# Reciprocal decays from one reciprocal and a backward scan, in a linear-attention, MLP and expert kernel

## The chip, the cores and the metric

One core of a Trainium2 chip runs the whole program. The metric is the device time of one execution in microseconds (us); lower is better. PE is TensorE (matmul), PEld its weight loads, DVE is VectorE, ACT is ScalarE, POOL is GpSimd, SP is the engine that issues most of the DMA transfers.

## The reference

The attention part keeps a state per head and decays it by `w` at every position; two feed-forward parts follow. Only the first part is touched by the change.

```
for t in range(S):                       # S = 768, batch 4, 8 heads, 48 wide
    kt, vt, rt, wt = (k[:, :, t], v[:, :, t], r[:, :, t], w[:, :, t])
    cur = np.einsum('bhd,bhe->bhde', u[None] * kt, vt)
    y[:, :, t] = np.einsum('bhd,bhde->bhe', rt, state + cur)
    state = wt[:, :, :, None] * state + np.einsum('bhd,bhe->bhde', kt, vt)
...
h = x @ w_in                             # 3072 x 384 times 384 x 2048
x = (np.maximum(h, 0.0) + alpha * np.minimum(h, 0.0)) @ w_out
...                                      # then the best of 8 experts per token: relu(x @ w1) @ w2, times its gate weight
```

## The kernel before, in words

**Attention by tiles.** The 3072 tokens are 24 tiles of 128 positions, six to a batch element. Inside a tile the recurrence is turned into matmuls: with the running product of decays `ex` (one per position, head and channel), `r` is multiplied by `ex`, `k` is divided by the `ex` of the position behind it, and the masked product of the two gives the scores. The 112 partitions of `dm` are two heads of 48 channels with a gap of 16, and along each partition lie four head pairs: 512 values of `r`, 512 of `k` and then `w` as four runs of 129, the first of each run being 0, so that one scan over 516 values starts anew in every run.

For a tile DVE does `scan` (L277, writes `ex`), `rec0` (L301, the reciprocal of every fourth `ex`), `rec1` (L305, three multiplications that get the other three of four, each from the one behind it times `w`), and `k` (L307, `k` times `rec`). POOL does `r` (L292, `r` times `ex`), the product `rk` (L312 and then L313), the masks of the scores (L360), and further on `cv` (L328) and the state's decay (L395). DVE sums `rk` to `c` (L318), adds `y` and `cv` to `x` (L424), and splits `x` into a high and a low part (L446 writes the low one, `xtl`).

**Blocks.** Three tiles make a block of 384 tokens for the first MLP: 16 steps, each nine matmuls into `ph` (L584, of which two buffers exist), ACT's `gn` (L587), DVE's `gt` (L589), ACT's `gh` (L595), DVE's `gl` (L597) and nine matmuls into `py` (L610). While a block goes through its 16 steps, the tiles of the next block are done between them.

**Weights.** `w_in` and `w_out` arrive as 64-bit words in 16 pieces. Each piece takes three DVE instructions of 768 columns (L207, L208, L211), two of ACT (L203, L224), and a subtraction for the low part (L229, on DVE for even pieces, which writes `wil`, on POOL for odd ones, `wol`). This work runs in the prologue and in the first MLP block alone.

**What sets the order.** The prologue (tiles 0 to 2 and the first pieces of weights) is written out by hand for all engines, by a table of times (`PRO_OPS`, `PRO_MOVED`) that gives nothing but an order. From the first MLP step on only PE's order is written by hand; a scheduler that estimates durations orders DVE, ACT, POOL and SP. From six steps before the last MLP step on, DVE's order is by hand as well.

Of the kernel before, what the change touches and what calls it, by code (L numbers as in the profile page):

```python
# [9 lines left out]
F32 = mybir.dt.float32  # L10
# [16 lines left out]
NP = H // 2  # L27
PR = 112
KC = DM // 128
NF1 = DFF // 128  # L30
# [32 lines left out]
OPS = {  # L63
# [6 lines left out]
PRO_OPS = {  # L70
# [3 lines left out]
}  # L74
PRO_NEXT = ("scan", "rec0", "rec1", "k", "r", "rk")
PRO_MOVED = {
# [6 lines left out]
}  # L83
# [13 lines left out]
def attention_mlp_moe(ctx, tc, dmaj, tmaj, ub, alpha, w_in, w_out, w_gate, w_gate_b, wexp, out):  # L97
# [23 lines left out]
    def load_tile(i):  # L121
        if i < NB:
            both = wp.tile([128, 1540 + 3 * DM], F32, tag="W", name="both")
            dm, tm = both[:PR, :1540], both[:, 1540:].rearrange("p (c d) -> p c d", c=3)
            if i == 0:
                sp.dma_start(out=dm[:, 1024:], in_=dmaj[i, :, 1024:])
                sp.dma_start(out=dm[:, :1024], in_=dmaj[i, :, :1024])
            else:
                sp.dma_start(out=dm, in_=dmaj[i])
        else:  # L130
            dm = ap.tile([PR, 1540], F32, tag="dm", name="dm")
            tm = ap.tile([128, 3, DM], F32, tag="tm", name="tm")
            sp.dma_start(out=dm, in_=dmaj[i])
# [19 lines left out]
    pool.memset(apat, 0.0)  # L153
    pool.memset(apat[:, :, 0:1], 1.0)
    ident = cst.tile([128, 128], F32, name="ident")
    make_identity(nc, ident)
# [108 lines left out]
    def att_tile(i, s0):  # L265
# [8 lines left out]
        def scan():  # L274
# [3 lines left out]
                out=ex.rearrange("p a t -> p (a t)"),  # L278
                data0=dm[:, 1024:1540],
                data1=apat.rearrange("p a t -> p (a t)"),  # L280
# [7 lines left out]
            cx["v"] = tm_t[i][:, 2, :]  # L288
            cx["rec"] = ap.tile([PR, NP, 128], F32, tag="rec", name="rec", bufs=1)

# [3 lines left out]
        def rec(n):  # L294

            def at4(t, m):
                return t.rearrange("p a (g m) -> p a g m", m=4)[:, :, :, m]

            rc, ex = cx["rec"], cx["ex"][:, :, 1:129]
            if n == 0:  # L300
                vec.reciprocal(out=at4(rc, 3), in_=at4(ex, 3))  # L301
            elif n == 1:
                w = dm_t[i][:, 1024:1540].rearrange("p (a t) -> p a t", a=NP)[:, :, 1:129]
                for m in (2, 1, 0):
                    vec.tensor_tensor(out=at4(rc, m), in0=at4(rc, m + 1), in1=at4(w, m + 1), op=ALU.mult)  # L305
            else:
                vec.tensor_tensor(out=cx["k"], in0=cx["k"], in1=rc, op=ALU.mult)  # L307

# [134 lines left out]
        def x_low():  # L443
# [4 lines left out]
        ops = {  # L448
            "scan": scan, "r": decay_r, "rec0": lambda: rec(0), "rec1": lambda: rec(1), "k": lambda: rec(2),
            "rk": diag, "c": diag_sum, "cv": diag_v, "sc": scores,  # L450
# [642 lines left out]
```

## Time and profile before

| | us |
|---|---|
| three timed runs, median (lowest to highest) | 880.32 (878.28 to 882.1) |
| the profiled execution, its own time | 875.71 |
| its span, first to last instruction | 874.0 |
| PE busy, share of the span | 820.5 (94%) |
| DVE busy | 645.4 (74%) |
| ACT busy | 384.3 (44%) |
| POOL busy | 293.4 (34%) |

The shares are means over stages with different limits: a prologue up to about 43 us, the first MLP block with the weights' work up to about 147 us, the other MLP blocks up to about 550 us, and the experts after that. Where an instruction waits inside its engine for something that is not a semaphore, the profile shows it as a longer duration, not as idle time.

### The profile page before, as it was taken

What the parts mean: (1) busy time and instruction counts of PE and PEld (TensorE: products, weight loads), DVE (VectorE), ACT (ScalarE), POOL (GpSimd) and SP (SyncE); (2) the same over time, 40 slices, a digit from 0 to 9 for tenths busy, and PEclk for the clock granted to TensorE, in tenths of its full rate; (3) what the DMA queues carried; (4) which work ended last, traced back from release to release, by engine and by line L of the source; (5) the groups of instructions that cost most, each with busy time, mean ns of one, the idle gap of its engine ahead of it and who ended that gap; (6) DMA issues with size and microseconds to landing.
All of it is one profiled execution on the core that took longest, in us unless ns stands there. A gap on an engine that the chain in (4) does not pass through costs nothing. (4 is left out here: it accounts for less than half of the span.)

```text
span 874.0 us, 14602 instructions
## 1 busy us (share of the span) xinstructions
PE 820.5 (94%) x5453; PEld 796.1 (91%) x5453; DVE 645.4 (74%) x1219; ACT 384.3 (44%) x751; POOL 293.4 (34%) x309
## 2 busy tenths in 40 slices
PE   6878789999799999999999999999999999999994
PEld 4768779999799999999999999999899999999993
DVE  6999898977686996896996983446767576776761
ACT  3545343344133433333333432337355556565641
POOL 5474444233332433343423330122224122232301
PEclk8779888999899999999999999999999999999997
DMA  9625534022212321311312300036456668585830
GB/s 281 203 83 171 193 120 148 29 60 86 59 59 60 87 60 60 86 60 60 86 60 59 87 1 1 28 137 242 147 202 240 224 216 293 204 294 204 275 119 21
DMA packets 30513, 111.59 MB, mean 128 GB/s; under 512 B 8229, under 2 KB 11592, under 8 KB 30440
## 3 DMA queue, kind: packets, MB, share of 16 engines
q1 hardware_dynamic: 26088, 100.38, 35.8%
q0 software_dynamic: 4352, 10.26, 3.2%
q8 instruction: 44, 0.72, 0.3%
q14 instruction: 29, 0.24, 0.1%
HBM read 100.95 MB, written 10.45 MB: 127 GB/s over the span
## 5 line engine op out<-in xcount | busy, mean ns | idle before, releaser
L584 PE MATMUL ph<-xth,wih 128*128 128x384 f32 x384 | 138.1, 360 | 8.4 <-DVE gt L589 5.2
L610 PE MATMUL py<-woh,gh 128*128 128x384 f32 x384 | 138.1, 360 | 1.0 <-ACT gh L595 1.0
L584 PE MATMUL ph<-xth,wil 128*128 128x384 f32 x384 | 132.9, 346 | 6.2 <-DVE wil L229 6.2
L595 ACT CAST gh<-gt 128x384 fp32r<-128x384 f32 x128 | 65.6, 513 | 158.5 <-DVE gt L589 158.5
L610 PE MATMUL py<-woh,gl 128*128 128x384 f32 x384 | 131.4, 342 | 1.4 <-DVE gl L597 1.4
L584 PE MATMUL ph<-xtl,wih 128*128 128x384 f32 x384 | 132.3, 345 | 0.0
L610 PE MATMUL py<-wol,gh 128*128 128x384 f32 x384 | 131.2, 342 | 0.0
L597 DVE TENSOR_TENSOR gl<-gt,gh 128x384 fp32r<-128x384 f32 x128 | 91.9, 718 | 33.3 <-ACT gh L595 31.8
L589 DVE SCALAR_TENSOR_TENSOR gt<-gn,oma_s,ph 128x384 f32<-128x384 f32 x128 | 76.4, 597 | 50.3 <-ACT gn L587 50.1
L587 ACT ACTIVATE gn<-ph 128x384 f32<-128x384 f32 x128 | 62.7, 490 | 113.2 <-PE ph L584 110.1
L815 DVE SCALAR_TENSOR_TENSOR gl<-ph,gh 128x256 fp32r<-128x256 f32 x96 | 40.4, 422 | 73.9 <-ACT gh L813 67.2
L489 DVE SCALAR_TENSOR_TENSOR sink<-x,wgb 128x384 f32<-128x384 f32 x144 | 88.1, 634 | 2.1 <-ACT x L621 1.4
L584 PEld LDWEIGHTS ph<-xth,wih 128*128 128x128 f32 x384 | 74.6, 194 | 10.3 <-DVE gt L589 5.8
L810 PE MATMUL ph<-xh,w1h 128*128 128x256 f32 x288 | 81.5, 283 | 1.2 <-DVE gl L815 1.1
L584 PEld LDWEIGHTS ph<-xth,wil 128*128 128x128 f32 x384 | 74.7, 194 | 7.4 <-DVE wil L229 7.4
L884 POOL DMA_INDIRECT out<-ys,meta x28 | 28.5, 1018 | 156.3 <-ACT ys L881 97.5
L810 PE MATMUL ph<-xl,w1h 128*128 128x256 f32 x288 | 80.8, 281 | 0.0
L810 PE MATMUL ph<-xh,w1l 128*128 128x256 f32 x288 | 80.4, 279 | 0.0
L610 PEld LDWEIGHTS py<-woh,gh 128*128 128x128 f32 x384 | 74.7, 195 | 3.0 <-ACT gh L595 1.3
L610 PEld LDWEIGHTS py<-woh,gl 128*128 128x128 f32 x384 | 74.1, 193 | 2.5 <-DVE gl L597 2.5
L584 PEld LDWEIGHTS ph<-xtl,wih 128*128 128x128 f32 x384 | 74.9, 195 | 0.8 <-DVE xtl L446 0.3
L610 PEld LDWEIGHTS py<-wol,gh 128*128 128x128 f32 x384 | 74.6, 194 | 0.0
(211 smaller groups left out, 1906.4 us busy)
## 6 DMA issues: line engine op xcount, KB each, us to landing
raw<-w SPq DMA_DIRECT2D x64, 768.0 KB
dm<-dmaj SPq DMA_DIRECT2D x21, 673.8 KB
tm<-tmaj SPq DMA_DIRECT2D x21, 576.0 KB
raw<-w_out SPq DMA_DIRECT2D x8, 768.0 KB
raw<-w_in SPq DMA_DIRECT2D x7, 768.0 KB
x2d<-x SPq DMA_DIRECT2D x8, 576.0 KB
both<-tmaj SPq DMA_DIRECT2D x3, 576.0 KB
wgb<-w_gate_b SPq DMA_DIRECT2D x2, 768.0 KB
```

The lines of the kernel that those rows point to most:

```text
L489: vec.scalar_tensor_tensor(out=sink, in0=x2[:, j, :], scalar=1.0, in1=wgb_t[h][:, e, :], op0=ALU.mult, op1=ALU.mult, accum_out=cx["l"][:, ...
L584: pe.matmul(ph, lhsT=w, rhs=x[:, c, :], start=k == 0, stop=k == 3 * KC - 1)
L587: act.activation(gn, ph, AF.Relu, scale=-1.0)
L589: vec.scalar_tensor_tensor(out=gt, in0=gn, scalar=oma_s[:, f : f + 1], in1=ph, op0=ALU.mult, op1=ALU.add)
L595: act.copy(gh, gt)
L597: vec.tensor_tensor(out=gl, in0=gt, in1=gh.bitcast(F32), op=ALU.subtract)
L610: pe.matmul(y_t[blk][j], lhsT=g[:, sl], rhs=w, start=f == 0 and m == 0, stop=f == NF1 - 1 and m == 2,)
L810: pe.matmul(ph, lhsT=w, rhs=x, start=k == 0, stop=k == 3 * KC - 1)
L815: vec.scalar_tensor_tensor(out=gl, in0=ph, scalar=0.0, in1=gh.bitcast(F32), op0=ALU.max, op1=ALU.subtract)
L884: pool.indirect_dma_start(out=out, out_offset=bass.IndirectOffsetOnAxis(ap=d["meta"][:, j, 0:1], axis=0), in_=ys, in_offset=None, bounds_c ...
```

## The change

The other reciprocals of a tile no longer come from every fourth position. One reciprocal of four values (the last `ex` of each of the four runs) goes into a tile `inj` that is zero elsewhere, and a second scan runs from the end to the front: `rec[t] = w[t+1] * rec[t+1] + inj[t]`. It needs `w` one position further, so `dm` grows by one column (1541 instead of 1540). `inj` is filled with zeros once, by POOL, at the start. Where `rec0` and `rec1` stood at two places of the hand-written order, everything is now at that of `rec0`.

```diff
-    "scan": -9, "r": -9, "rec0": -7, "rec1": -5, "k": -3, "rk": -6, "c": 0, "cv": 0, "sc": 0,
+    "scan": -9, "r": -9, "rec0": -7, "k": -3, "rk": -6, "c": 0, "cv": 0, "sc": 0,
...
-    (3, "scan"): 19.55, (3, "rec0"): 19.58, (3, "rec1"): 21.52, (3, "k"): 21.54,
+    (3, "scan"): 19.55, (3, "rec0"): 19.58, (3, "k"): 21.54,
...
+    inj = ap.tile([PR, NP, 129], F32, tag="inj", name="inj", bufs=1)
+    pool.memset(inj, 0.0)
...
             if n == 0:
-                vec.reciprocal(out=at4(rc, 3), in_=at4(ex, 3))
-            elif n == 1:
-                w = dm_t[i][:, 1024:1540].rearrange("p (a t) -> p a t", a=NP)[:, :, 1:129]
-                for m in (2, 1, 0):
-                    vec.tensor_tensor(out=at4(rc, m), in0=at4(rc, m + 1), in1=at4(w, m + 1), op=ALU.mult)
+                vec.reciprocal(out=inj[:, :, 128], in_=ex[:, :, 128])
+                vec.tensor_tensor_scan(
+                    out=rc.rearrange("p a t -> p (a t)")[:, ::-1],
+                    data0=dm_t[i][:, 1025 : 1025 + NP * 129][:, ::-1],
+                    data1=inj.rearrange("p a t -> p (a t)")[:, ::-1],
+                    initial=0.0,
+                    op0=ALU.mult,
+                    op1=ALU.add,
+                )
             else:
-                vec.tensor_tensor(out=cx["k"], in0=cx["k"], in1=rc, op=ALU.mult)
+                vec.tensor_tensor(out=cx["k"], in0=cx["k"], in1=rc[:, :, 1:129], op=ALU.mult)
```

PE's order is the same instruction for instruction. The orders of DVE and POOL move from the first MLP block on, where the scheduler sets them. In the lists below a scan appears as SCALAR_TENSOR_TENSOR, and the lines of the changed kernel are four or five higher (L281 is the forward scan, L302 the reciprocal, L303 the backward scan, L312 `k`, L323 `c`, L429 `x`).

The first place is DVE in the prologue, at tile 3; `x` here is that of tile 1, and `v` is a piece of weights. Before:

```order
L277 SCALAR_TENSOR_TENSOR ex<-dm,apat 112x516
L301 RECIPROCAL rec<-ex 112x128
L424 TENSOR_TENSOR x<-py,cv 128x384
L207 TENSOR_SCALAR v_380<-v_380 128x768
L208 SCALAR_TENSOR_TENSOR v_380<-raw,v_380 128x768
```

In the changed kernel, at the same place:

```order
L281 SCALAR_TENSOR_TENSOR ex<-dm,apat 112x516
L302 RECIPROCAL inj<-ex 112x4
L303 SCALAR_TENSOR_TENSOR rec<-dm,inj 112x516
L429 TENSOR_TENSOR x<-py,cv 128x384
L211 TENSOR_SCALAR v_377<-v_377 128x768
```

The backward scan stands ahead of `x` of tile 1; the three L305 of this tile stood further down, behind `x` of tile 2, and are gone there.

The second place is DVE at the start of the first MLP block, at tile 4; `gt` and `gl` are those of the first MLP step. Before:

```order
L318 TENSOR_REDUCE c<-rk 128x8
L277 SCALAR_TENSOR_TENSOR ex<-dm,apat 112x516
L229 TENSOR_TENSOR wil_119<-v_454,wih_118 128x3x256
L207 TENSOR_SCALAR v_496<-v_496 128x768
L301 RECIPROCAL rec<-ex 112x128
L208 SCALAR_TENSOR_TENSOR v_496<-raw,v_496 128x768
L589 SCALAR_TENSOR_TENSOR gt<-gn,oma_s,ph 128x384
L211 SCALAR_TENSOR_TENSOR v_496<-raw,v_496 128x768
L597 TENSOR_TENSOR gl<-gt,gh 128x384
L207 TENSOR_SCALAR v_537<-v_537 128x768
L305 TENSOR_TENSOR rec<-rec,dm 112x128
```

In the changed kernel, from the same `c` (that of tile 3) on:

```order
L323 TENSOR_REDUCE c<-rk 128x8
L281 SCALAR_TENSOR_TENSOR ex<-dm,apat 112x516
L233 TENSOR_TENSOR wil_121<-v_448,wih_120 128x3x256
L211 TENSOR_SCALAR v_490<-v_490 128x768
L302 RECIPROCAL inj<-ex 112x4
L323 TENSOR_REDUCE c<-rk 128x8
L212 SCALAR_TENSOR_TENSOR v_490<-raw,v_490 128x768
L211 TENSOR_SCALAR v_531<-v_531 128x768
L594 SCALAR_TENSOR_TENSOR gt<-gn,oma_s,ph 128x384
L215 SCALAR_TENSOR_TENSOR v_490<-raw,v_490 128x768
L602 TENSOR_TENSOR gl<-gt,gh 128x384
L212 SCALAR_TENSOR_TENSOR v_531<-raw,v_531 128x768
```

The `c` of tile 4 has come forward, from right behind the MLP's seventh `gt` to right behind the reciprocal: it and the next piece's L211 now stand ahead of the first `gt`. POOL's order is the same up to that point; behind the backward scan, which is the next row, `gt` of the second step follows.

The third place is DVE further on in the first MLP block, ahead of `wil` of the piece that the ninth MLP step needs (the first `c` is that of tile 4, the second that of tile 5). Before:

```order
L589 SCALAR_TENSOR_TENSOR gt<-gn,oma_s,ph 128x384
L208 SCALAR_TENSOR_TENSOR v_742<-raw,v_742 128x768
L318 TENSOR_REDUCE c<-rk 128x8
L211 SCALAR_TENSOR_TENSOR v_742<-raw,v_742 128x768
L597 TENSOR_TENSOR gl<-gt,gh 128x384
L277 SCALAR_TENSOR_TENSOR ex<-dm,apat 112x516
L318 TENSOR_REDUCE c<-rk 128x8
L229 TENSOR_TENSOR wil_739<-v_742,wih_738 128x3x256
```

In the changed kernel, up to the same `wil` (the `c` is that of tile 5):

```order
L323 TENSOR_REDUCE c<-rk 128x8
L212 SCALAR_TENSOR_TENSOR v_734<-raw,v_734 128x768
L602 TENSOR_TENSOR gl<-gt,gh 128x384
L215 SCALAR_TENSOR_TENSOR v_734<-raw,v_734 128x768
L303 SCALAR_TENSOR_TENSOR rec<-dm,inj 112x516
L312 TENSOR_TENSOR dm<-dm,rec 112x512
L211 TENSOR_SCALAR v_772<-v_772 128x768
L233 TENSOR_TENSOR wil_731<-v_734,wih_730 128x3x256
```

The forward scan of tile 5 has left this place for an earlier one, its `c` stands seven rows ahead of `wil` instead of right before it, and the backward scan and `k` of tile 5 stand here instead.

## Rows read from the trace of the kernel before

**Rows 1.** Busy us (x instructions) of PE, PEld, DVE, ACT, POOL; clock; DMA share; GB/s

```profile
12.00:43.00 31.00, 23.73 (x154) 20.48 (x153) 29.38 (x36) 15.25 (x47) 15.47 (x15) 0.75 0.81 245
43.00:147.00 104.00, 84.82 (x470) 80.22 (x469) 97.17 (x120) 48.20 (x89) 54.69 (x50) 0.83 0.41 138
147.00:550.00 403.00, 396.94 (x2656) 387.49 (x2655) 313.20 (x729) 144.64 (x335) 137.51 (x158) 0.99 0.21 61
```

**Rows 2.** PE's waits from 43 to 147 us: total us, times, longest us

```profile
PE ph L584 <- DVE wil L229: 6.2, 3, 5.0
PE ph L584 <- DVE gt L589: 4.5, 1, 4.5
PE px L435 <- DVE x L424: 3.9, 2, 3.4
```

**Rows 3.** Instructions around tile rec, whole span: ns min/median/max, first and last start

```profile
L305 DVE TENSOR_TENSOR rec<-rec,dm x63: 373/391/1402, 39.3 to 507.4; 112x128 f32<-112x128 f32 x63
L301 DVE RECIPROCAL rec<-ex x24: 937/955/957, 5.0 to 503.9; 112x128 f32<-112x128 f32 x24
```

**Rows 4.** Instructions of line 277, the forward scan, in the same columns

```profile
L277 DVE TENSOR_TENSOR_SCAN ex<-dm,apat x21: 1210/1223/1855, 30.7 to 500.4; 112x516 f32<-112x516 f32 x21
```

**Rows 5.** Instructions of line 549, a small reciprocal of the gate

```profile
L549 DVE RECIPROCAL g_meta<-g_se x8: 177/178/179, 177.0 to 622.7; 128x3 f32<-128x3 f32 x8
```

**Rows 6.** Timeline at tile 1: start, us, engine, line [idle before <-releaser]

```profile
13.21 0.96 DVE L301 RECIPROCAL rec<-ex 112x128 f32<-112x128 f32 x1
13.26 1.18 POOL L292 TENSOR_TENSOR both<-both,ex 112x512 f32<-112x512 f32 x1 [1.80 <-DVE ex L277]
...
14.20 2.70 DVE L305 TENSOR_TENSOR rec<-rec,both 112x128 f32<-112x128 f32 x3
...
14.39 1.15 POOL L312 TENSOR_TENSOR rk<-both 128x384 f32<-128x384 f32 x1
15.62 1.03 POOL L313 TENSOR_TENSOR rk<-rk,ub_s 128x384 f32<-128x384 f32 x1
...
17.28 0.68 DVE L307 TENSOR_TENSOR both<-both,rec 112x512 f32<-112x512 f32 x1
...
18.35 0.54 DVE L318 TENSOR_REDUCE c<-rk 128x8 f32<-128x384 f32 x1
```

**Rows 7.** Timeline at tile 3, the last of the prologue's scans

```profile
31.98 0.96 DVE L301 RECIPROCAL rec<-ex 112x128 f32<-112x128 f32 x1
32.03 1.18 POOL L292 TENSOR_TENSOR dm<-dm,ex 112x512 f32<-112x512 f32 x1 [1.19 <-DVE ex L277]
32.85 0.49 DVE L424 TENSOR_TENSOR x<-py,cv 128x384 f32<-128x384 f32 x1
33.16 1.00 POOL L312 TENSOR_TENSOR rk<-tm 128x384 f32<-128x384 f32 x1
...
33.40 0.55 PE L435 MATMUL px<-ident,x 128*128 128x128 f32 x3 [2.02 <-DVE x L424]
```

**Rows 8.** Timeline at tile 4, the start of the first MLP block

```profile
50.27 0.94 DVE L301 RECIPROCAL rec<-ex 112x128 f32<-112x128 f32 x1
...
51.93 0.60 DVE L589 SCALAR_TENSOR_TENSOR gt<-gn,oma_s,ph 128x384 f32<-128x384 f32 x1
...
52.45 4.88 DVE L211 SCALAR_TENSOR_TENSOR v<-raw,v 128x768 uint32<-128x768 uint32 x1
...
54.93 0.99 POOL L313 TENSOR_TENSOR rk<-rk,ub_s 128x384 f32<-128x384 f32 x1
```

**Rows 9.** DVE's groups, 43 to 147 us: busy us, mean ns | idle before <-releaser

```profile
L211 DVE SCALAR_TENSOR_TENSOR v<-raw,v 128x768 uint32<-128x768 uint32 x13 | 19.6, 1511 | 0.0
...
L207 DVE TENSOR_SCALAR v<-v 128x768 uint32<-128x768 uint32 x14 | 9.6, 688 | 0.9 <-ACT v L203 0.8
L305 DVE TENSOR_TENSOR rec<-rec,dm 112x128 f32<-112x128 f32 x12 | 7.2, 597 | 0.1
...
L318 DVE TENSOR_REDUCE c<-rk 128x8 f32<-128x384 f32 x5 | 2.7, 544 | 2.5 <-POOL rk L313 2.5
...
L211 DVE SCALAR_TENSOR_TENSOR v<-spare,v 128x768 uint32<-128x768 uint32 x1 | 1.0, 959 | 0.0
```

More of the change, by code (lines that the diff above doesn't have):

```diff
@@ L28 @@
 PR = 112
+DMW = 2 * 512 + NP * 129 + 1
 KC = DM // 128
@@ L74 @@
 }
-PRO_NEXT = ("scan", "rec0", "rec1", "k", "r", "rk")
+PRO_NEXT = ("scan", "rec0", "k", "r", "rk")
 PRO_MOVED = {
[1 row of a table removed]
[1 row of a table added]
     (2, "sc"): 15.7, (2, "ktr"): 15.82, (2, "a0"): 15.84, (2, "a1"): 15.9, (2, "ko"): 16.0, (1, "cv"): 16.1,
@@ L122, in load_tile @@
         if i < NB:
-            both = wp.tile([128, 1540 + 3 * DM], F32, tag="W", name="both")
-            dm, tm = both[:PR, :1540], both[:, 1540:].rearrange("p (c d) -> p c d", c=3)
+            both = wp.tile([128, DMW + 3 * DM], F32, tag="W", name="both")
+            dm, tm = both[:PR, :DMW], both[:, DMW:].rearrange("p (c d) -> p c d", c=3)
             if i == 0:
@@ L130, in load_tile @@
         else:
-            dm = ap.tile([PR, 1540], F32, tag="dm", name="dm")
+            dm = ap.tile([PR, DMW], F32, tag="dm", name="dm")
             tm = ap.tile([128, 3, DM], F32, tag="tm", name="tm")
@@ L278, in scan @@
                 out=ex.rearrange("p a t -> p (a t)"),
-                data0=dm[:, 1024:1540],
+                data0=dm[:, 1024 : 1024 + NP * 129],
                 data1=apat.rearrange("p a t -> p (a t)"),
@@ L288, in scan @@
             cx["v"] = tm_t[i][:, 2, :]
-            cx["rec"] = ap.tile([PR, NP, 128], F32, tag="rec", name="rec", bufs=1)
+            cx["rec"] = ap.tile([PR, NP, 129], F32, tag="rec", name="rec", bufs=1)
         def decay_r():
@@ L294, in rec @@
         def rec(n):
-            def at4(t, m):
-                return t.rearrange("p a (g m) -> p a g m", m=4)[:, :, :, m]
-            rc, ex = cx["rec"], cx["ex"][:, :, 1:129]
+            rc, ex = cx["rec"], cx["ex"]
             if n == 0:
-                vec.reciprocal(out=at4(rc, 3), in_=at4(ex, 3))
-            elif n == 1:
-                w = dm_t[i][:, 1024:1540].rearrange("p (a t) -> p a t", a=NP)[:, :, 1:129]
-                for m in (2, 1, 0):
-                    vec.tensor_tensor(out=at4(rc, m), in0=at4(rc, m + 1), in1=at4(w, m + 1), op=ALU.mult)
+                vec.reciprocal(out=inj[:, :, 128], in_=ex[:, :, 128])
[7 more added lines that the diff above has]
+                )
             else:
-                vec.tensor_tensor(out=cx["k"], in0=cx["k"], in1=rc, op=ALU.mult)
+                vec.tensor_tensor(out=cx["k"], in0=cx["k"], in1=rc[:, :, 1:129], op=ALU.mult)
         def diag():
@@ L448, in att_tile @@
         ops = {
-            "scan": scan, "r": decay_r, "rec0": lambda: rec(0), "rec1": lambda: rec(1), "k": lambda: rec(2),
+            "scan": scan, "r": decay_r, "rec0": lambda: rec(0), "k": lambda: rec(1),
             "rk": diag, "c": diag_sum, "cv": diag_v, "sc": scores,
@@ L1049, in pairs @@
         return t.reshape(NTILE, 2, D, NP, 128)
-    dmaj = np.zeros((NTILE, PR, 2 * 512 + 516), np.float32)
-    dw = dmaj[:, :, 1024:].reshape(NTILE, PR, NP, 129)
+    dmaj = np.zeros((NTILE, PR, DMW), np.float32)
     dw = np.zeros((NTILE, PR, NP, 129), np.float32)
@@ L1060 @@
         dw[:, sl, :, 1:] = ww[:, j]
-    dmaj[:, :, 1024:] = dw.reshape(NTILE, PR, 516)
+    dmaj[:, :, 1024 : 1024 + NP * 129] = dw.reshape(NTILE, PR, NP * 129)
     def tmj(x):
```

4 rows, old and new, of tables (PRO_MOVED, PRO_OPS) are left out of this document.

## The prediction

> **What bounds the kernel now.** I read the busy times by stage first. From 147 to 550 us PE is busy for 396.94 of 403 us at a granted clock of 0.99; DVE has 90 us to spare there [rows 1]. So whatever the change saves on DVE after about 147 us, 16 of the 24 tiles, is hidden under the matmuls, and no attention is left in the stage of the experts. What can move is the prologue (12 to 43 us, DVE busy 29.38 of 31) and the first MLP block (43 to 147 us, DVE busy 97.17 of 104, PE only 84.82 at a clock of 0.83) [rows 1]. PE's waits in that block name DVE: 6.2 us for `wil`, 4.5 for `gt`, 3.9 for `x` [rows 2].
>
> Then I asked what DVE's 97 us are made of, because the same instruction has very different lengths. L211 takes 0.959 us on one piece and 1.511 on the mean of 13 others; L305 has a median of 391 ns, but a mean of 597 in this block [rows 3, 9]. The timelines show why. L211 at 52.45 us lasted 4.88 us, until just after POOL's chain of `cv`, `rk`, `r` and `rk` was over; its last `rk` ended at 55.92 [rows 8]. At tile 1 the three L305 took 2.70 us, as long as POOL's three instructions beside them, while the reciprocal at 13.21, beside POOL's L292, took its usual 0.96 [rows 6]. So a DVE instruction that reads two tensors from SBUF does not run while POOL works on SBUF, and a reciprocal does. The Trainium skill has this rule (SBUF — State Buffer, section SBUF: two separate sides): DVE and GpSimd share a pair of ports, and whichever starts first holds it for its whole instruction. The trace agrees, with 4.88 us against 0.96.
>
> **What the change removes and adds.** Per tile it removes a reciprocal of 0.955 us (L301) and three L305 of 0.391, 2.13 us together [rows 3]. It adds a reciprocal of four values and a scan over 516. For the first the nearest row is the gate's reciprocal of three values, 0.178 us [rows 5]. For the second it is the forward scan over as many values, 1.223 us [rows 4]. No row shows an instruction that reads backwards. It could cost the same (nothing but the sign of the step differs) or, as an upper bound, twice as much, 2.4 us. I take 1.223, since L305 reads every fourth value and its median of 391 ns shows no such price. Added are then 1.40 us, and 0.73 are saved by durations. Neighbours overlap by about 0.09 us in the timeline (the reciprocal at 50.27 plus 0.94 ends after its follower would have begun, [rows 8]), so two instructions fewer save 0.18 less: **0.55 us per tile**. The memset of `inj`, the column that `dm` gains (4 bytes in 6160) and the longer `rec` are priced at nothing: POOL waits 1.80 us before its first work on tile 1 alone [rows 6], and if that cover were gone they cost some tenths of a us once.
>
> What matters more: the new scan reads two tensors from SBUF, the long reciprocal one. POOL could work under the reciprocal; it can't under the scan.
>
> **Prologue.** At tile 1 L292 starts at 13.26, 0.05 us after the old reciprocal [rows 6]. The new one ends at about 13.21 + 0.18 = 13.39, too late to be first, so the scan waits until L292 ends at 14.44 and runs to about 15.7. L312 follows (1.0, to 16.7), then `k` or L313. `k` can end at 17.3 instead of 17.96, but `c` of tile 1 needs L313, which moves from 16.65 to about 18.3: `c` stays at 18.35 [rows 6], and so does all that DVE does behind it. Taken: 0; bounds -1.7 (the two parts of `rec` shrink from 3.66 to 1.4 plus a wait of at least 0.5) and +0.3. Tile 2 has the same pattern; I take -0.7 for `k`, on which PE waits, bounds -2 and +0.3.
>
> At tile 3 L292 starts at 32.03, again 0.05 after the reciprocal [rows 7]. The scan then waits until 33.21 and ends at about 34.4, and `x` of tile 1, which PE already waits for (2.02 us, [rows 7]), is behind it: 34.3 for 32.85, **+1.4**. If the scan comes first, +0.45. The three L305 that go behind `x` of tile 2 (1.2 us) are worth 0, because the `xtl` behind them waits for the transposes of that very `x` anyhow. Prologue: -0.7 + 1.4 = **+0.7 us**, between -3 and +2.
>
> **First MLP block**, tiles 4 to 7.
> - DVE's own time: 4 x 0.55 = -2.2.
> - Waits of L305 for POOL: 7.2 - 12 x 0.391 = 2.5 us [rows 3, 9], which go. The four new scans wait in their place; POOL is busy 54.69 of 104 us [rows 1], and one of its instructions takes about 1.1 [rows 6, 7]: from 0 to 4 x 1.1 = 4.4, taken 4 x 0.4 = 1.6. Together -0.9.
> - The `c` of tile 4 now stands ahead of the first `gt`, and needs the `rk` that ended at 55.92 [rows 8]. The scheduler believed it ready; the trace says it isn't. DVE gets to it at about 50.27 + 0.18 = 50.5. POOL, undisturbed meanwhile, may be done a us earlier, at 54.9. So DVE idles 4.4 us (3.5 to 5.4) where it lost 4.88 - 0.96 = 3.9 inside L211 before: +0.5. What queues behind it: `gt` of the first step moves from 51.93 to about 54.9 + 0.54 + 0.96 + 0.69 = 57.1 (`c`, a piece's L208 priced as L211, and L207, [rows 9]), and PE, which waited 4.5 us for it, waits about 9.7. PE's 5.2 us are given back if DVE is not behind by then, for PE was to stop 3.4 us for `x` and 5.0 for `wil` further on [rows 2], and both come earlier in DVE's list now: ahead of `x` two L305 and a `gt` less, ahead of `wil` no `c` that has just to wait.
> - That wait for `rk` was 2.5 us [rows 9]; its `c` now has more work ahead of it: -1, between -2.5 and 0.
> - What POOL did under four reciprocals, 4 x 0.955 x 54.69/104 = 2.0 us, it now does at the cost of some other two-tensor instruction: +2.0, between 0 and 3.8.
>
> Block: -2.2 - 0.9 + 0.5 - 1 + 2.0 = **-1.6 us**. With the prologue -0.9 of the profiled 875.71. The timed median is 880.32, 4.6 above the profiled run, so on its scale 879.4; I say **879 us**. A measurement of this kernel can tell about 0.5%, 4.4 us, from no change.
>
> **Rivals.**
> 1. *DVE's list sets the block, and POOL finds other holes* (faster). For it: DVE is in line without a gap for nearly all of 12 to 147 us. Against it: the share of its time that is waiting for POOL. Then the +2.0 falls away, the wait for `rk` goes entirely (-1.5 more), and at tile 3 the scan starts before POOL (+0.45 for +1.4, about -1 more): -0.9 - 2.0 - 1.5 - 1 = -5.4, **875 us**.
> 2. *The wait at `c` of tile 4 stays* (slower). PE's extra 5.2 us are not given back, because `x` and `wil` are late by as much as PE is. It decides from the point where PE reaches the transposes of that `x` later than before: -0.9 + 5.2 = +4.3, **884.6 us**, and more if the `rk` of later tiles repeats it. For it: nothing shortens POOL's chain. Against it: by the bullet above DVE itself is only 0.5 us behind at that place.
> 3. *The backward scan takes twice as long* (slower): 1.2 us more for each of eight tiles, +9.8 on the forecast, **889 us**. Against it: L305's steps. The skill leaves it open (Vector Engine (DVE) Microarchitecture Reference, section 5.1, lists how an operand with a negative step streams as not measured); no run here shows it yet.
>
> **How the numbers follow.** Forecast 0.45, rival 1 0.34, rival 2 0.16, rival 3 0.05. The scheduler's new order from 43 us on makes each of these wide, some 4 us either way. Below the forecast the range takes in rival 1 with that width, to 871. Above it reaches past rival 2, to 886, and leaves out most of rival 3. Faster by over 0.5% is rival 1, 0.34; slower is rivals 2 and 3, 0.21; the rest 0.45.
>
> **What would show it.** Right: the new reciprocal at about 0.18 us; the backward scan at 1.2 where POOL is silent and 2 or more behind L292 at tiles 1 to 3; DVE idle 4 us for POOL's `rk` at about 50 us and PE waiting 9 us for `gt`; the waits for `x` and `wil` shorter; from about 150 us on the same PE time, with DVE some 9 us less busy (16 x 0.55). Wrong: a backward scan of 2.4 us everywhere; scans that start ahead of L292; a first MLP block that is over 4 us shorter or longer; a new wait of PE after 150 us, where the order moved too and I count on none.

## The result, and the profile after

The changed kernel takes **890.55 us** (median of four runs, 889.81 to 891.26) against 879.77 for the kernel before on the same chip: a ratio of **1.0125**, 95% interval 1.0106 to 1.0145, 10.8 us slower. The prediction was 879 us, between 871 and 886, with "no change" as the likeliest. A few executions in a slower state are left out of all medians and ratios.

The profiled execution took 891.26 us with a span of 889.4. That of before took 875.71, below its own median, so the two traces lie 15.4 us apart in span where the medians differ by 10.8. There is one trace of each kernel, so it stays open in which stage the other executions differ from them. In what follows the lines of the changed kernel are some five further on: L302 is the small reciprocal, L303 the backward scan, L281 the forward one, L296 `r`, L317 and L318 `rk`, L323 `c`, L594 `gt`, L451 `xtl`, L589 the matmuls of `ph`.

First the busy time by stage, in the columns of [rows 1].

```profile
12.00:43.00 31.00, 24.16 (x149) 20.74 (x149) 27.23 (x30) 14.56 (x44) 17.87 (x15) 0.73 0.79 243
43.00:147.00 104.00, 77.23 (x457) 72.03 (x455) 90.86 (x110) 45.47 (x85) 53.34 (x48) 0.87 0.41 138
147.00:550.00 403.00, 385.60 (x2573) 374.95 (x2572) 310.07 (x686) 141.98 (x329) 147.41 (x157) 0.99 0.22 61
```

The last line is the surprise. PE was busy for 396.94 us of this stage before; now it is idle for 11.3 us more. PE's waits in this stage (total us, times, longest) say for what:

```profile
PE ph L589 <- DVE xtl L451: 10.9, 5, 2.4
PE px L440 <- DVE x L429: 5.7, 1, 5.7
PE ph L589 <- DVE gt L594: 0.7, 1, 0.7
```

The kernel before has one wait of PE here, 6.1 us for `x`. New are the waits for `xtl`: five, and one more of 1.5 at 142.69, just ahead of this stage. All six are at the second matmul of a new MLP block. The new instructions over the whole span (ns minimum/median/maximum), to set beside [rows 3]:

```profile
L303 DVE TENSOR_TENSOR_SCAN rec<-dm,inj x21: 1221/2161/3133, 30.5 to 519.2; 112x516 f32<-112x516 f32 x21
L303 DVE TENSOR_TENSOR_SCAN rec<-both,inj x3: 1233/2102/4231, 5.2 to 18.7; 112x516 f32<-112x516 f32 x3
L302 DVE RECIPROCAL inj<-ex x24: 164/181/185, 5.0 to 518.3; 112x4 f32<-112x4 f32 x24
```

A backward scan that nobody disturbs takes 1.22 us, like the forward one [rows 4]; the median is 2.16. The timeline at one of the block starts (start, us, engine, line, [idle before <-releaser]) puts both findings together:

```profile
282.56 0.18 DVE L302 RECIPROCAL inj<-ex 112x4 f32<-112x4 f32 x1
282.66 1.19 POOL L296 TENSOR_TENSOR dm<-dm,ex 112x512 f32<-112x512 f32 x1 [2.03 <-PE px L440]
...
282.78 3.12 DVE L303 TENSOR_TENSOR_SCAN rec<-dm,inj 112x516 f32<-112x516 f32 x1
...
283.81 1.00 POOL L317 TENSOR_TENSOR rk<-tm 128x384 f32<-128x384 f32 x1
...
284.13 0.42 PE L589 MATMUL ph<-xth,wih 128*128 128x384 f32 x1
284.89 1.80 POOL L318 TENSOR_TENSOR rk<-rk,ub_s 128x384 f32<-128x384 f32 x1
285.82 0.58 DVE L594 SCALAR_TENSOR_TENSOR gt<-gn,oma_s,ph 128x384 f32<-128x384 f32 x1
286.33 0.54 DVE L451 TENSOR_TENSOR xtl<-px,xth 128x384 fp32r<-128x384 f32 x1
...
286.93 0.44 PE L589 MATMUL ph<-xtl,wih 128*128 128x384 f32 x1 [2.38 <-DVE xtl L451]
```

And DVE, POOL and one weight load of PE in the kernel before at the same place of the program:

```profile
279.01 0.96 DVE L301 RECIPROCAL rec<-ex 112x128 f32<-112x128 f32 x1
279.11 1.19 POOL L292 TENSOR_TENSOR dm<-dm,ex 112x512 f32<-112x512 f32 x1 [2.02 <-PE px L435]
279.89 0.51 DVE L589 SCALAR_TENSOR_TENSOR gt<-gn,oma_s,ph 128x384 f32<-128x384 f32 x1
280.32 0.55 DVE L446 TENSOR_TENSOR xtl<-px,xth 128x384 fp32r<-128x384 f32 x1
...
280.79 0.74 DVE L305 TENSOR_TENSOR rec<-rec,dm 112x128 f32<-112x128 f32 x1
...
280.92 0.19 PEld L584 LDWEIGHTS ph<-xtl,wih 128*128 128x128 f32 x1 [0.18 <-DVE xtl L446]
```

Before, `r` of POOL ran beside the long reciprocal; when that was over, `gt` and `xtl` were ready and came next, and the three multiplications that read two tensors from SBUF came later. Even so the weight load behind `xtl` sat idle for 0.18 us: there was nothing to spare. Now the reciprocal is over in 0.18 us, ACT's `gn` is not yet done, and the scheduler puts the backward scan there. It waits through POOL's `r` and first `rk` (1.9 us of its 3.12), and `gt` and `xtl` queue behind it. The tile in question is the second one of the next block. I call tiles 4, 7, 10, 13, 16, 19 and 22 the middle tiles; the five waits from 147 us on belong to the last five of them.

The wait at 142.69 has another cause. There the scan of tile 7 stands behind `xtl`:

```profile
138.63 1.89 DVE L602 TENSOR_TENSOR gl<-gt,gh 128x384 fp32r<-128x384 f32 x1 [0.79 <-ACT gh L600]
...
142.10 0.54 DVE L451 TENSOR_TENSOR xtl<-px,xth 128x384 fp32r<-128x384 f32 x1
...
143.31 2.04 DVE L303 TENSOR_TENSOR_SCAN rec<-dm,inj 112x516 f32<-112x516 f32 x1
```

What is late is `gl`, which runs beside POOL's subtraction for `wol` (138.26, 1.84 us), and the forward scan behind it. That is the order in which DVE comes out of the first MLP block. A wait of 1.3 to 2.4 us at this place is in every experiment below but 3, 4 and 10 (0.8 in 4), whichever form tile 7 has.

The six waits are 12.5 us by the page of the profile. Behind the last one (492.45) the granted clock is 0.50 from 494 to 497 us, the lower of the two levels (1.2 GHz), where the kernel before had 1.00 from 470 to 500 us; that is 1.5 us more. Progress of PE, read at the same transposes `px` in both traces, agrees: 0.5 us behind at 138 us, 2.3 at 160, 6.0 at 300, 8.8 at 390, 11.2 at 432, 15.2 at 499, and no more after that.

### The profile page after: what moved, and what is told of

Read it like the earlier page. It is cut to its first block, busy times and chain, and to the rows that moved or that the text cites. A ratio compares the mean times of both kernels' runs of the same rounds, so it can differ in the third digit from the quotient of the medians.

```text
span 889.4 us, 14552 instructions
## 1 busy us (share of the span) xinstructions
PE 817.3 (92%) x5453; PEld 790.9 (89%) x5453; DVE 640.9 (72%) x1171; ACT 383.3 (43%) x751; POOL 308.6 (35%) x310
## 5 line engine op out<-in xcount | busy, mean ns | idle before, releaser
L589 PE MATMUL ph<-xth,wih 128*128 128x384 f32 x384 | 137.4, 358 | 18.2 <-DVE gt L594 11.1
L589 PE MATMUL ph<-xtl,wih 128*128 128x384 f32 x384 | 131.9, 343 | 12.5 <-DVE xtl L451 12.5
L589 PE MATMUL ph<-xth,wil 128*128 128x384 f32 x384 | 132.4, 345 | 5.8 <-DVE wil L233 5.8
L594 DVE SCALAR_TENSOR_TENSOR gt<-gn,oma_s,ph 128x384 f32<-128x384 f32 x128 | 77.4, 605 | 58.5 <-ACT gn L592 58.2
L589 PEld LDWEIGHTS ph<-xth,wih 128*128 128x128 f32 x384 | 74.2, 193 | 20.9 <-DVE gt L594 12.0
L494 DVE SCALAR_TENSOR_TENSOR sink<-x,wgb 128x384 f32<-128x384 f32 x144 | 91.0, 658 | 1.9 <-ACT x L626 1.4
L589 PEld LDWEIGHTS ph<-xtl,wih 128*128 128x128 f32 x384 | 74.3, 193 | 14.1 <-DVE xtl L451 14.1
L589 PEld LDWEIGHTS ph<-xth,wil 128*128 128x128 f32 x384 | 74.2, 193 | 7.3 <-DVE wil L233 7.3
```

Source lines behind the costliest of these rows:

```text
L494: vec.scalar_tensor_tensor(out=sink, in0=x2[:, j, :], scalar=1.0, in1=wgb_t[h][:, e, :], op0=ALU.mult, op1=ALU.mult, accum_out=cx["l"][:, ...
L589: pe.matmul(ph, lhsT=w, rhs=x[:, c, :], start=k == 0, stop=k == 3 * KC - 1)
L594: vec.scalar_tensor_tensor(out=gt, in0=gn, scalar=oma_s[:, f : f + 1], in1=ph, op0=ALU.mult, op1=ALU.add)
```

## The experiments

Each ran on the chip beside the kernel before. "xtl" and "x" are the waits of `ph` for `xtl` and of `px` for `x` from 147 to 550 us in the profiled execution.

| | median us | ratio (95%) | xtl | x |
|---|---|---|---|---|
| kernel before | | | 0 | 6.1 |
| changed kernel | 890.55 | 1.0125 (1.0106 to 1.0145) | 10.9 | 5.7 |
| 1 old form on the middle tiles | 880.07 | 1.0015 (0.9995 to 1.0036) | 0 | 6.2 |
| 2 new form on the middle tiles alone | 889.77 | 1.0135 (1.0108 to 1.0162) | 10.9 | 6.2 |
| 3 new form on tiles 0 to 3 alone | 879.29 | 1.0009 (0.9992 to 1.0025) | 0 | 8.6 |
| 4 DVE by hand for two steps of a block | 893.47 | 1.0164 (1.0138 to 1.0191) | 0 | 11.8 |
| 5 scan behind `gt` and `xtl` | 890.32 | 1.0120 (1.0097 to 1.0143) | 0 | 14.2 |
| 6 no products on POOL, middle tiles | 878.43 | 0.9978 (0.9956 to 1.0001) | 2.7 | 6.4 |
| 7 short reciprocal, no backward scan | see there | | 12.3 | 5.5 |
| 8 `r` behind the scan, middle tiles | 893.13 | 1.0181 (1.0148 to 1.0213) | 3.0 | 14.3 |
| 9 `r` behind the scan, from tile 3 on | 888.83 | 1.0116 (1.0084 to 1.0148) | 2.9 | 14.0 |
| 10 before, slot numbers later | 886.88 | 1.0073 (1.0048 to 1.0099) | 0.5 | 12.7 |
| 11 `r` behind scan and `rk` | 887.09 | 1.0083 (1.0055 to 1.0110) | 4.6 | 6.7 |

The kernel before took between 875 and 886 us over all these runs, so the times alone don't rank experiments that are a few us apart. The waits for `x` vary too: experiment 3, whose tiles from 4 on are those of the kernel before and whose time is the same, has 7.6 us in the third block and 1.0 in the fifth.

**Experiments 1 and 2: which tiles.** One kernel holds both forms of `rec`, and a condition on the tile's number `i` chooses.

```diff
-            if n == 0:
+            new = i % NB != 1 or i < NB      # experiment 1
+            new = i % NB == 1 and i >= NB    # experiment 2
+            if n == 0 and not new:
+                vec.reciprocal(out=at4(rc[:, :, 1:129], 3), in_=at4(ex[:, :, 1:129], 3))
...
```

> Tiles 4, 7, 10, 13, 16, 19 and 22 (the second tile of each block from the second block on) go back to the reciprocal of every fourth position and three multiplications; the other 17 tiles keep the one reciprocal and the backward scan. Theory A (the loss is made at the block starts, where the backward scan of just these tiles stands ahead of gt and xtl on VectorE and TensorE waits for xtl, 12.5 us in six waits, and a clock drop behind the last one costs about 1.5 us more): the waits of line 'ph <- VectorE xtl' fall from 12.5 us to under 1.5 us and the time from 890.5 to 875 to 879 us. Theory B (the loss comes from the other order of the attention's instructions in the first MLP block and the 17 other tiles' scans): the time stays above 885 us. Theory C (the backward scan costs VectorE more wherever it stands): the time lies between, at 883 to 887 us.

> The other half of the first experiment: only tiles 4, 7, 10, 13, 16, 19 and 22 have the one reciprocal and the backward scan, the other 17 tiles are as in the kernel before. Theory A: TensorE waits for xtl at six block starts as in the changed kernel, 10 to 13 us in all, and the time is 887 to 893 us. Theory B: 878 to 882 us. Theory C: 882 to 885 us.

The first is no different from the kernel before, though 17 tiles have the new form, and its waits for `xtl` after 147 us are gone; the one of the second block start is still there (1.72 us at 139.31), and its median is 1.1 us above the range I gave. The second has the whole loss with seven tiles. Theory A holds as to the place, for five of the six starts; B and C fall. Scans of other tiles wait as long (3.13 us at 263.1 in the changed kernel), and PE doesn't wait there.

**Experiment 3: the prologue alone.**

```diff
+            new = i <= NB
```

> Only tiles 0 to 3, whose decays are worked out before the first MLP block, have the new form; tiles 4 to 23 are as in the kernel before. It measures the prediction's term of the prologue (+0.7 us at its end, tile 2 gaining 0.7 and tile 3 losing 1.4) without anything behind it. Theory A: within 2 us of the kernel before, 878 to 882 us, and no wait for xtl at any block start after 150 us. Theory B or C: slower than before by 3 us or more.

No difference that can be measured, and no wait for `xtl` after 147 us. In its trace the transposes at 74 us come 0.7 us earlier than before and those at 138 us 0.5 later. The prediction's +0.7 for the prologue is too small for such a run to confirm or refute.

**Experiment 4: `gt` and `xtl` first, by hand.** DVE follows the written order in the first two steps of each block but the first.

```diff
+        if 0 < i < NM + SWITCH:
+            order.close()
+            order.enter_context(tc.manual_schedule(engines=ORDER2 if i >= NF1 and i % NF1 < 2 else ORDER1))
```

> All 24 tiles have the new form; in the first two steps of every MLP block but the first, VectorE's instructions are taken in the order in which the program is written, so that gt and xtl stand ahead of the next tile's forward scan, reciprocal and backward scan. Arithmetic as in the changed kernel. Theory A: the waits for xtl at block starts fall from 12.5 us to under 2 us and the time to 876 to 880 us. Theory C (the scan's hold only moves on): TensorE waits for gt, gl or px instead, together over 8 us more than before, and the time stays above 885 us.

The waits of `ph` for `xtl` went, the time did not: 893 us. PE waited 11.8 us for `x` (8.9 at 237.85), 3.5 in five pieces for ACT, and 1.3 for `xtl` at other places. By the time that is this experiment's theory C, though the waits for `x` grew by 5.7 us where it asks for 8; but the edit reorders all of DVE's work in those steps, the routing's and the sums `c` too, so it doesn't say what of it was the scan. The next one moves the scan alone.

**Experiment 5: the scan behind `xtl`.** The scheduler sees the scan's input later, because it goes through two copies on ACT.

```diff
-                vec.reciprocal(out=inj[:, :, 128], in_=ex[:, :, 128])
+                if i >= NB and i % NB == 1:
+                    vec.reciprocal(out=wide[:, :, 0], in_=ex[:, :, 128])
+                    act.copy(wide[:, :, 1], wide[:, :, 0])
+                    act.copy(inj[:, :, 128], wide[:, :, 1])
+                else:
+                    vec.reciprocal(out=inj[:, :, 128], in_=ex[:, :, 128])
```

> All tiles have the new form; on tiles 4, 7, 10, 13, 16, 19 and 22 the reciprocal's four numbers reach the backward scan through two copies on ScalarE, 112x4 each. VectorE has no more work than in the changed kernel, but the backward scan is ready later and now stands behind gt and xtl at the block starts; nothing else is reordered there except that c follows k. Arithmetic as in the changed kernel. Theory A (the place of the scan ahead of gt and xtl is the loss): the waits for xtl fall from 12.5 us to under 1.5 us and the time to 876 to 880 us. Theory C (the scan's hold only moves to gl, px or scores): other waits of TensorE after 150 us grow by 8 us or more and the time stays above 885 us.

Theory A as I had it fell here. The order is the wanted one, no wait for `xtl` is left after 147 us, and the time is the changed kernel's: theory C of this experiment came about. PE's waits in this stage:

```profile
PE px L446 <- DVE x L435: 14.2, 2, 9.2
PE ph L595 <- DVE gt L600: 0.7, 1, 0.7
PE py L425 <- POOL at L371: 0.3, 1, 0.3
```

The wait for `x` in the third block grew from 6.1 to 9.2, of which experiment 3 had 1.5 without any of this, and one of 5.06 us in the fifth is new. Behind the new one the granted clock is 0.50 from 379 to 386 us, where the kernel before has 1.00 from 360 to 390: PE, 8.0 us behind it ahead of that wait, is 15.6 us behind afterwards. What is behind `x` shows on POOL. First the kernel before, around the start of the fifth block, then experiment 5 at the same place:

```profile
347.39 1.52 POOL L313 TENSOR_TENSOR rk<-rk,ub_s 128x384 f32<-128x384 f32 x1
350.04 1.03 POOL L551 DMA_INDIRECT metad<-g_meta,g_slot  x1 [1.13 <-DVE g_slot L543]
354.20 0.96 POOL L551 DMA_INDIRECT metad<-g_meta,g_slot  x1 [3.12 <-DMA metad<-g_meta,g_slot]
...
358.06 1.19 POOL L551 DMA_INDIRECT metad<-g_meta,g_slot  x1 [1.06 <-DMA metad<-g_meta,g_slot]
362.40 0.18 POOL L548 COPY g_meta<-tokid 128x3 int32<-128x3 int32 x1 [3.15 <-DMA metad<-g_meta,g_slot]
362.54 1.02 POOL L395 TENSOR_TENSOR st<-st,pm 112x384 f32<-112x384 f32 x1
```

```profile
355.36 2.33 POOL L324 TENSOR_TENSOR rk<-rk,ub_s 128x384 f32<-128x384 f32 x1
359.66 1.03 POOL L562 DMA_INDIRECT metad<-g_meta,g_slot  x1 [1.97 <-DVE g_slot L554]
364.46 0.96 POOL L562 DMA_INDIRECT metad<-g_meta,g_slot  x1 [3.77 <-DMA metad<-g_meta,g_slot]
...
368.72 1.40 POOL L562 DMA_INDIRECT metad<-g_meta,g_slot  x1 [1.28 <-DMA metad<-g_meta,g_slot]
376.00 0.18 POOL L559 COPY g_meta<-tokid 128x3 int32<-128x3 int32 x1 [5.88 <-DMA metad<-g_meta,g_slot]
376.15 0.99 POOL L406 TENSOR_TENSOR st<-st,pm 112x384 f32<-112x384 f32 x1
```

This is a second chain that leaves the block start: DVE's `g_slot` (the routing of an earlier block), three indirect DMAs one after another on POOL, then the state's decay `st` behind them on the same engine; ACT's `pm` waits for `st`, and a `gn` stands behind `pm`, so that `gt`, `x` and at last PE wait. The first DMA starts 2.65 us after POOL's last product began before, 4.30 now: the scan behind `xtl` still waits for POOL, holds POOL's product up in turn (2.33 for 1.52 us), and `g_slot` now queues behind the scan. From the first DMA to `st` it then takes 16.5 us in place of 12.5.

**Experiment 6: the scan's wait by itself.** The order stays the changed kernel's; POOL's three products of the middle tiles are left out.

```diff
         def decay_r():
+            if i >= NB and i % NB == 1:
+                return
...
+            if i >= NB and i % NB == 1:
+                cx["rk"] = ub_s
+                return
```

> On tiles 4, 7, 10, 13, 16, 19 and 22 GpSimd's product r (r with the decays) and both its products for rk are left out, so that the scores of these tiles are made of undecayed r and their c of another tensor. VectorE's order at the block starts is the changed kernel's, with the backward scan ahead of gt and xtl. Theory A1 (of the 2.4 us that TensorE waits for xtl, the 1.9 us come from the scan's wait for GpSimd): the scan takes 1.2 us there in place of 3.1 us, the wait for xtl falls to 0.3 to 0.7 us a block, under 3.5 us in all, and the time to 879 to 884 us. Theory A2 (a 1.2 us scan ahead of gt and xtl is enough for most of it, whatever GpSimd does): the waits for xtl stay at 8 us or more and the time at 887 us or more.

Theory A1 holds: the scan takes 1.23 us there, and the waits for `xtl` are 0.47 to 0.72 us a block. PE is within 0.7 us of the kernel before at each of the transposes from 400 to 611 us, but that flatters it: at 138 us it was already 4.2 us ahead, with tile 4's products left out in the first MLP block too. From 138 to 499 us it loses 4.9 us where the changed kernel loses 14.7, and 1.9 of the 4.9 are at the second block start, the one with another cause. (Its routing differs, so only the time up to there is strictly comparable; the whole is 0.2% below before, 0.6 us under the range I gave.) So a scan of 1.2 us ahead of `gt` and `xtl` costs 0.5 us of waiting a block, and without POOL's products most of the rest of the loss is gone. The run can't tell the scan's wait from the relief of POOL itself, whose DMAs follow the products.

**Experiment 7: without any backward scan.** The kernel before, with a shorter reciprocal; the positions that it no longer fills keep a constant, filled in once by POOL at the start.

```diff
...
-                vec.reciprocal(out=at4(rc, 3), in_=at4(ex, 3))
+                vec.reciprocal(out=rc[:, :, 127], in_=ex[:, :, 127])
```

> The kernel before, with its three multiplications and no backward scan; only the reciprocal is cut from 128 numbers of each partition to the four at the tile's ends, and the other 124 positions keep a constant, so that k is scaled by other numbers. With the reciprocal short the scheduler puts two of the three multiplications ahead of gt and xtl at the block starts. Theory A (the short reciprocal, by what it lets move ahead of gt and xtl, makes the loss; a backward scan isn't needed for it): TensorE waits 0.7 to 2.4 us for xtl at six block starts, 4 to 12 us in all, and the time is 882 to 889 us. Theory D (it takes the backward scan to lose time): no wait for xtl after 150 us of over 0.4 us, and the time is 874 to 880 us.

PE's waits from 147 to 550 us, and DVE at one of the block starts:

```profile
PE ph L586 <- DVE xtl L448: 12.3, 5, 2.7
PE px L437 <- DVE x L426: 5.5, 1, 5.5
```

```profile
276.61 0.18 DVE L303 RECIPROCAL rec<-ex 112x4 f32<-112x4 f32 x1
276.83 3.39 DVE L307 TENSOR_TENSOR rec<-rec,dm 112x128 f32<-112x128 f32 x2
280.14 0.61 DVE L591 SCALAR_TENSOR_TENSOR gt<-gn,oma_s,ph 128x384 f32<-128x384 f32 x1
280.66 0.55 DVE L448 TENSOR_TENSOR xtl<-px,xth 128x384 fp32r<-128x384 f32 x1
```

The same loss at the same places, with two of the old multiplications (3.39 us for what takes 0.39 each undisturbed [rows 3]) where the scan stood. The waits are 1.7 to 2.7 us each, a little more than the 0.7 to 2.4 I gave. Theory A holds. Its whole time, 927.67 us, is no measure: k of another size routes the tokens differently, and PE then does 5579 matmuls instead of 5453. Up to the last routing matmul (631.56 against 621.40 us) it is 10.2 us behind the kernel before, with 24 shorter reciprocals; at 138 us it was 7.1 us ahead, so from there on it loses more than the changed kernel.

**Experiments 8 and 9: all of POOL's work, but `r` later.**

```diff
+            if i >= NB and i % NB == 1:      # experiment 9: i >= NB
+                pool.tensor_scalar(cx["ex"][:, 0, 0:1], cx["rec"][:, 0, 0:1], 0.0, 1.0, op0=ALU.mult, op1=ALU.add)
...
```

In the written order, too, `r` stands behind the backward scan here.

> The changed kernel with all its work; on tiles 4, 7, 10, 13, 16, 19 and 22 GpSimd's product r is made to wait for the backward scan (by one more GpSimd instruction on a single number, which writes the 1.0 that r's decays begin with again and reads the scan's result first). VectorE's order at the block starts is the changed kernel's, with the backward scan ahead of gt and xtl; on GpSimd the first product of rk now stands ahead of r. Theory A1 (the loss is the scan's wait for GpSimd's products, and it strikes whatever stands behind the scan): the scan takes 1.2 to 2.0 us at the block starts in place of 3.1, the waits for xtl fall from 12.5 us to 3 to 7 us, and the time to 877 to 884 us. Theory A2 (a scan ahead of gt and xtl loses the time whatever GpSimd does): waits for xtl of 10 us or more and a time of 887 us or more.

> The eighth experiment's edit on all tiles from tile 3 on, not only on the seven at the block starts. Theory A1, with the block starts alone counting: the same time as the eighth experiment, within 2 us, and mean durations of the backward scan near 1.3 us in place of 2.2. If the wait for GpSimd costs time at the other tiles too, it is faster than the eighth experiment by 2 us or more; if r, now later, keeps the scores waiting, TensorE waits for r (line of the scores) appear and it is slower.

The first half came out, the time did not. A block start of experiment 8:

```profile
206.66 1.23 DVE L305 TENSOR_TENSOR_SCAN rec<-dm,inj 112x516 f32<-112x516 f32 x1
207.81 0.59 DVE L596 SCALAR_TENSOR_TENSOR gt<-gn,oma_s,ph 128x384 f32<-128x384 f32 x1
208.32 0.55 DVE L453 TENSOR_TENSOR xtl<-px,xth 128x384 fp32r<-128x384 f32 x1
...
211.99 0.55 DVE L325 TENSOR_REDUCE c<-rk 128x8 f32<-128x384 f32 x1 [1.96 <-POOL rk L320]
...
212.67 0.16 DVE L550 TENSOR_TENSOR g_slot<-g_pos,g_mi 128x3 int32<-128x3 f32 x1
```

The scan runs undisturbed in 1.23 us and PE waits 0.49 us for `xtl`, near what experiment 6 has. But POOL's three products now end later, `c` waits 1.96 us for `rk`, and `g_slot` is behind it. The waits for `x` are 9.4 and 4.9 us, as in experiment 5, and the time is 893 us. In experiment 9 the scans of this stage take 1.34 us on the mean, as expected. It is 4.3 us faster than 8, which by what I wrote would speak for the other tiles' waits; but in the traces PE is 3.7 us ahead of 8 from 138 to 204 us and only 1.3 at 542, so the lead was made in the first MLP block. What made it there is open.

**Experiment 10: the second chain by itself.** The kernel before, with DVE's order as it was, and one copy on POOL ahead of the indirect DMAs of five blocks.

```diff
+            if blk < NBLK - 3:
+                wide = ap.tile([128, nt, 192], I32, tag="wide", name="wide", bufs=1)
+                pool.tensor_copy(wide, slot.to_broadcast([128, nt, 192]))
+                slot = wide
...
-                    out_offset=bass.IndirectOffsetOnAxis(ap=slot[:, j, :], axis=0),
+                    out_offset=bass.IndirectOffsetOnAxis(ap=slot[:, j, 0:1], axis=0),
```

> The kernel before, all of its arithmetic; for the routing of the first five blocks one GpSimd copy (slot numbers spread to 128x576) stands between g_slot and the three indirect DMAs, so that these start 1 to 2 us later at five block starts, with VectorE's order unchanged and no backward scan. It tests the second chain that the fifth and eighth experiment point to (g_slot, three indirect DMAs one after another, st behind them on GpSimd, then ScalarE, VectorE's x and TensorE's px). Theory F (that chain has next to no slack at the block starts): the wait for x of 6 us in the third block grows to 8 to 10 us, one of 3 to 6 us appears in the fifth, and the time is 884 to 891 us. Theory G (it has slack, and the waits for x in experiments 5 and 8 come from elsewhere): waits for x within 1.5 us of the kernel before, time under 882 us.

Theory F holds, by the time of 886.88 us and by the wait of 4.88 us for `x` in the fifth block. That of 7.85 us in the third (8 to 10 expected) is no sign, since experiment 3 has 7.6 there. The wait in the fifth is again followed by the lower clock, 0.50 from 373 to 379 us: PE falls 7.5 us behind there, 4.9 by the wait and about 2.6 by the clock. The copy took 0.76 us:

```profile
351.06 0.76 POOL L546 COPY wide<-g_slot 128x576 int32<-128x576 int32 x1 [0.93 <-DVE g_slot L543]
352.10 1.17 POOL L555 DMA_INDIRECT metad<-g_meta,wide  x1 [0.28 <-POOL wide L546]
356.89 0.96 POOL L555 DMA_INDIRECT metad<-g_meta,wide  x1 [3.61 <-DMA metad<-g_meta,wide]
...
369.14 0.99 POOL L395 TENSOR_TENSOR st<-st,pm 112x384 f32<-112x384 f32 x1
```

Counted from the block's last transposes (344.65 us before, 345.89 here), the first DMA starts 0.8 us later and `st` 5.4 us later. The traces show what the DMAs run beside. The store of a block's `x2d` (576 KB) is issued at 357.34, 0.45 us after the second of them, and that one takes 5.2 us until the third starts. At the same block the second had a lead of 2.85 us on the store in the kernel before (357.05) and took 3.9; in experiment 8 a lead of 0.73 us, and 6.1; in 9 a lead of 0.48, and 5.4. Against it stands experiment 5, where the store came 0.30 us ahead of the second and that took 4.3, and the third, which met a tile's load, 7.3. The third of them fits better. In experiments 5, 8, 9 and 10 the tile's load that follows the store is issued between 0.01 us before it and 0.78 us after, and it takes 6.4 to 7.3 us until POOL goes on; in the kernel before and in experiment 11 it has a lead of 3.4 us and takes 4.3 and 4.1. That transfers of half a megabyte hold the small ones up is still a reading of these places: no run varied it alone, and what DVE and POOL do meanwhile wasn't held fixed either.

**Experiment 11: `r` last.** As 9 from tile 4 on, with `r` waiting for `rk` too, and written behind it.

```diff
+            if i >= NB + 1:
+                pool.tensor_tensor(
+                    out=cx["ex"][:, 0, 0:1], in0=cx["rec"][:, 0, 0:1], in1=cx["rk"][:PR, 0:1], op=ALU.mult
+                )
+                pool.tensor_scalar(cx["ex"][:, 0, 0:1], cx["ex"][:, 0, 0:1], 0.0, 1.0, op0=ALU.mult, op1=ALU.add)
...
```

> As the ninth experiment (from tile 4 on), but r waits for rk's second product too, so that GpSimd does both products of rk first and r last, with two instructions on single numbers ahead of r; VectorE's c then need not wait for r. Theory P (GpSimd's own queue of three products ahead of the first indirect DMA sets its start): the DMA starts within 0.6 us of the ninth experiment's, the waits for x stay near 9 and 4.5 us, and the time is 885 to 891 us. Theory Q (VectorE's wait for rk in c, with g_slot behind it, sets it): the DMA starts 1.5 us earlier, the wait in the fifth block falls under 1 us and the time is 876 to 882 us.

The time (887) is in P's range, its waits are not: 6.7 us for `x` in the third block and none in the fifth, but 0.54 to 1.56 us for `xtl` at five starts. With PE standing still there the next store comes later too (362.84, 2.84 us behind the second DMA), and from the first DMA (355.98) to `st` it is 12.4 us again. That DMA starts 6.68 us behind the transposes of its block, 7.05 in experiment 9: within P's 0.6. P and Q are not told apart by the time, then, since Q's condition never came about. So a delay by the one chain can cover the other's.

No version beat the kernel before. Experiments 1, 3 and 6 equal it, and 6 leaves work out.

## Why the prediction was wrong

**What held.** The new reciprocal takes 0.181 us (0.178 taken), the backward scan 1.22 us (1.223 taken) where POOL is silent, and 2.10, 4.23 and 2.10 at tiles 1 to 3; rival 3 is out. At tile 3 `x` was to be 1.4 us later behind the reciprocal. It starts 2.24 us behind it (30.31 and 32.55) where it was 0.87 [rows 7], and PE's wait for it grew from 2.02 to 3.43. At tile 4 `c` waits for `rk` and `gt` is late:

```profile
54.71 0.55 DVE L323 TENSOR_REDUCE c<-rk 128x8 f32<-128x384 f32 x1 [3.93 <-POOL rk L318]
...
56.51 0.61 DVE L594 SCALAR_TENSOR_TENSOR gt<-gn,oma_s,ph 128x384 f32<-128x384 f32 x1
```

3.93 us for the 4.4 forecast; PE waited 9.38 us for `gt`, 9.7 forecast. The 5 us more were made up, against rival 2: the transposes at 74.15 us before come at 74.66, and at 138 us PE is 0.5 us behind, where I had it 0.9 ahead.

**What came out by luck.** They were not made up in the way that I forecast. The waits for `wil` and `x` in this block fell from 6.2 and 3.9 [rows 2] to 5.8 and 2.3, which is 2.0 us, and those for ACT's `wih`, which the sum doesn't have, rose from 3.1 to 7.1. Between the transposes at 40 and those at 138 us PE waits 25.2 us in place of 19.1. What made up for that is the clock: for the same 420 matmuls PE was busy 73.59 us in place of 79.48, at a granted clock of 0.85 for 0.80 on the mean. Up to the transposes at 74 us one stretch shows it: the clock is 0.50 up to about 61 us in both traces, and PE worked through that from 52.58 on before, but only from 57.17 on in the changed kernel. So all the terms of the sum together were off by 1.4 us at 138 us, and by 3.2 with the wait at 142.69, but the clock, which is no term of it, moved 5.9 us of PE's time, and one trace of each kernel doesn't show how often it falls so.

**The step that failed** is none of those terms but the bound ahead of them: "whatever the change saves on DVE after about 147 us ... is hidden under the matmuls", and then "from about 150 us on the same PE time". The 90 us that DVE has to spare from 147 to 550 us are a sum over the stage. At each block start there are none (the weight load that waited 0.18 us at 280.92): within some 5 us of `xth` DVE owes PE `gt` and `xtl` and owes POOL `g_slot`, and the decays of a middle tile stand among them. I argued for savings, and forgot that a stage average hides a shorter instruction, but not a longer one at the place where PE is waiting.

**Which price I had, and left in the wrong stage.** I wrote that POOL could work under the long reciprocal and can't under the scan, and charged it to the first MLP block alone (+2.0 us there, as DVE's time). In the later blocks the 16 scans took 37.8 us (mean 2.36) where 19.6 would do, so DVE was not 9 us less busy but 3.1 (313.20 to 310.07). Five of those scans stood ahead of `gt` and `xtl` and became 10.9 us of PE's time, and 1.5 more by the clock. Experiments 1 and 2 show the place, 6 that the loss goes with POOL's products beside the scan, 7 that the shorter reciprocal is enough to cause it.

**What of the mechanism is shown.** That DVE and POOL standing in each other's way at the block starts makes the loss: experiments 1, 2, 6 and 7. That it goes through `xtl` in the changed kernel: of the 14.7 us that PE loses there from 138 to 499 us, the waits for `xtl` are 12.5, 1.5 of them with another cause, and the clock behind the last is 1.5. That `xtl` is not the only exit: 5 and 8, where the loss went through `g_slot` and the indirect DMAs instead, and 10, which makes it there alone. That is why moving the scan or `r` gave nothing back. Not shown apart is how much of experiment 6's gain is the scan's and how much POOL's, nor why the traces lie 4.6 us further apart than the medians. The list in the prediction of what would prove it wrong had "a new wait of PE after 150 us, where the order moved too and I count on none"; it was never given a price.

## What to carry to other kernels

Ask of a hidden engine not how much it has to spare in a stage, but what it owes, and to whom, at the moments when the bound engine changes work; a tile or block boundary is read in the timeline, not in a sum. A long instruction that another engine can work under is a cover as well as a cost: when a shorter one that can't run beside that engine takes its place, the wait comes out, and a scheduler that goes by ready times puts it ahead of what matters. When a fix clears one wait and the time stays, look for the second chain that leaves the same place before giving up the theory.

## What the runs showed of the hardware

- A DVE instruction that waits for POOL isn't always let in at POOL's next instruction. At 282.78 the scan waited through L296 and the L317 behind it, which doesn't depend on it, and ran before L318, which needs L317's result and then took 1.80 us instead of 1.0. At 351.31 it was let in right behind L296, took 2.16 us, and L317 took 1.92.
- The backward direction of a scan costs nothing that shows: 1.221 us at the least for 516 values, against 1.217 at the least and 1.226 on the median for the forward scan.
- PE's clock fell after one of six waits of 1.4 to 2.4 us, the one at 492.45, and not after the others: 0.50 granted from 494 to 497 us, and 1.00 in 205 to 225, 280 to 295 and 423 to 440, which hold three waits of the same 2.38 us. It was down behind waits for `x` as well: in the kernel before 0.50 from 234 to 237 us, where PE went on at 233.40 after 6.06 us, and in experiment 10 0.50 from 373 to 379, where it went on at 373.99 after 4.88.
- Three small indirect DMAs in a row took 12.5 us from the first to the state's decay behind them in the kernel before, and 16.4 to 17.0 in experiments 5, 8, 9 and 10, where the first started 0.8 to 1.7 us later behind its block's transposes. In experiment 11 it started 1.3 us later and they took 12.4 all the same.
